# Linear attention and two mixtures of experts on one core: the old state joins the sum on TensorE, and the flag's marks are formed two steps before they are summed

## The chip, the cores and the metric

The kernel runs on one core of a Trainium2 chip. The metric is the device time of one execution in microseconds (us), the median of several runs. A core has five engines with one queue each: TensorE (PE, matrix products; its weight loads are listed as PEld), VectorE (DVE), ScalarE (ACT), GpSimd (POOL) and SyncE (SP, which issues most transfers). Each works through its queue in order and waits there for semaphores of the others.

## The reference

Three stages follow each other. Sizes: 2 batches, 8 heads, 768 positions, head width 48; 1536 tokens of width 384.

```
# attention with a decaying state, per batch and head
state = alpha[t, :, None] * state + outer(k[t], v[t])
y[t]  = q[t] @ state
# one expert of 8 for each token (384 -> 1024 -> 384), gate = softmax at the maximum
e = argmax(x @ w_gate);  out = gate * (relu(x @ w1[e]) @ w2[e])
# a dense layer (384 -> 2048 -> 384); its weights come as 64-bit floats
h = x @ w_in;  out = (h * tanh(softplus(h))) @ w_out
```

## The kernel before, in words

All instructions are put on the engines' queues in the order in which the program text issues them; no planner moves them.

**Attention.** The 1536 tokens are cut into 12 tiles of 128 positions, six for each batch (`NC_B` is 6). A loop over the tiles is software-pipelined: pass i of the loop works on several tiles at once. Below, "round i" is pass i. What round i puts on the engines:

- DVE: two of the four scans of tile i+2 (the running products of alpha, L429), the state update of tile i-1 (`state_up`, L565, L566 or L568), the other two scans, then the scaled keys and queries of tile i+1 (L466, L470), two products for tile i+2 (L448, L453, which wait for the reciprocal `r` that ACT makes from the scans), and sums for the routing. After the tiles of a group (tiles 0 to 3, 4 to 6, 7 and 8) some ten to fourteen short operations for the routing of the group come on top, in rounds 4 and 5, 7 and 8, 9 and 10.
- ACT: copies of the scores (L487), logarithm and exponential of the scans (L438, L443), the negated transposed keys `kpn` (L503), copies of results.
- POOL: the causal mask on the scores (L488).
- PE: the scores of tile i (L483), the transposes of its keys (L497), the selection and gate products of tile i-1 (L547), the product of the queries with the carried state (`attend_state`, L518), the product with the masked scores (`attend_tile`, L529), and last the new part of the state (`state_mm`, L555), eight products of keys and values into the bank `bk[7]`, which wait for `kpn`.

The carried state is `s2f`/`s2` (112 partitions by 192 values, two heads on the partitions of each of four columns of heads). In the kernel before, `state_mm(i)` writes only the new part to PSUM, and `state_up(i)`, in the next round, adds the old state to it (L565) and multiplies the sum by the tile's decay (L566). For the first tile of a batch (tiles 0 and 6) there is no old state, and one multiplication does (L568). The last tile of a batch (5 and 11) has no state update. So L565 and L566 run 8 times, for tiles 1 to 4 and 7 to 10.

**Experts.** 64 steps (8 experts, 8 parts of the hidden width each) follow. A step puts on PE nine products of the first layer (`g1`, L1011) and nine of the second layer for the step three before it (`g2`, L1028); ACT and DVE turn the first layer's result into a high and a low part (`hh` L1015, `hl` L1016). Beside this, weights are split into high and low parts (`whi` on ACT, L319; `wlo` on DVE, L325), and the 64-bit weights of the dense layer are turned into 32-bit ones (`cvt_a`, `cvt_b`), with a mark in `unfit` for any value that can't be. At the end of step 60 `cvt_marks` forms one number from all marks: DVE takes the maximum per partition (L234) and compares it with zero (`mk`, L235), PE sums `mk` over the partitions into `bk[0]` (L236), and DVE joins the sum with another flag into `slow_i` (L237), which after everything else decides whether a slow exact path runs (it doesn't here).

**Dense layer.** Its first products (`f1`, L1091) are interleaved with the experts' last three steps, 61 to 63, and write the banks 0, 1, 4 and 5 in turn; the fourth `f1`, in bank 5, comes after the experts' last `g2`. ACT's `sigma` and `cosine` (L1103, L1107, L1109) and DVE's `gated` (L1117 to L1119) follow, then the second products (`f2`, L1132).

Of the kernel before, what the change touches and what calls it, by code (L numbers as in the profile page):

```python
# [12 lines left out]
BF16 = mybir.dt.bfloat16  # L13
# [3 lines left out]
ALU = mybir.AluOpType  # L17
# [6 lines left out]
def kernel(  # L24
# [18 lines left out]
    nc = tc.nc  # L43
    ctx.enter_context(tc.manual_schedule())
    B, H, S, D = q.shape
    NT, DM = out.shape
    E = w1.shape[0]
# [3 lines left out]
    NC_B = S // C  # L51
    NTILE = NT // C
    HP = H // 2
    HS = 64
    R2 = HS + D
    SW = 2 * D + E
    KD = DM // 128
    MF = FF // 128
# [169 lines left out]
        nc.sync.dma_start(out=cvt_jobs[n][1], in_=wt.bitcast(F32))  # L228


    def cvt_marks():
        mk = const.tile([128, 1], BF16, name="mk")
        mf = const.tile([128, 1], F32, name="mf")
        nc.vector.tensor_reduce(out=mf, in_=unfit, axis=AX.X, op=ALU.max)  # L234
        nc.vector.tensor_scalar(out=mk, in0=mf, scalar1=0.0, scalar2=None, op0=ALU.is_gt)  # L235
        nc.tensor.matmul(out=bk[0][:, 0:1], lhsT=ones, rhs=mk, start=True, stop=True)  # L236
        nc.vector.scalar_tensor_tensor(  # L237
            out=slow_i, in0=bk[0][0:1, 0:1], scalar=0.0, in1=slow_f, op0=ALU.is_gt, op1=ALU.max
        )


# [99 lines left out]
    with ExitStack() as actx:  # L341
# [44 lines left out]
        misc = bk[7]  # L386
# [162 lines left out]

        def state_mm(i):  # L550
            vn, kpn = vn_t[i], kpn_t.pop(i)
            for j in range(HP):
                for r in range(2):
                    p1 = min(R2, (r + 1) * HS)
                    nc.tensor.matmul(  # L555
                        out=kv[r * HS:p1, j, :], lhsT=kpn[:, j, r * HS:p1], rhs=vn[:, (2 * j + r) * D:(2 * j + r + 1) * D],
                        start=True, stop=True, skip_group_check=True,
                    )

        def state_up(i):  # L560
            pt = pt_t.pop(i)
            sv = s2[0:R2]
            dec = pt[0:R2, :, C - 1:C].to_broadcast([R2, HP, D])
            if i % NC_B:
                nc.vector.tensor_tensor(out=sv, in0=kv[0:R2], in1=sv, op=ALU.add)  # L565
                nc.vector.tensor_tensor(out=sv, in0=sv, in1=dec, op=ALU.mult)  # L566
            else:
                nc.vector.tensor_tensor(out=sv, in0=kv[0:R2], in1=dec, op=ALU.mult)  # L568

        LAST2 = NTILE - 2  # L570
        xg_l = [
# [668 lines left out]
    for e in range(E):  # L1240
        for m in range(MF):
# [29 lines left out]
                )  # L1271
            if step == E * MF - 4:
                cvt_marks()
            if m == 5 and e + 1 < E:
                xpose(e + 1)
                if e + 2 < E:
                    gather(e + 2)
# [240 lines left out]
```

## Time and profile before

| what | value |
|---|---|
| median of 3 runs | 449.08 us (448.35 to 450.48) |
| the profiled execution | 451.67 us, of which the span from first to last instruction is 449.8 us |
| mean granted clock of TensorE | 0.966 of full speed |
| PE busy | 420.8 us (94%) |
| DVE busy | 329.1 us (73%) |
| ACT busy | 330.9 us (74%) |
| attention, the loop over tiles | from the start to about 86 us |
| experts | about 95 to 240 us |
| dense layer | about 227 us to the end |

The attention stage is a mesh of short operations on four engines with waits on each; the two stages behind it are long rows of matrix products with PE hardly idle. PE's clock has two levels, 2.4 GHz and 1.2 GHz; the profile gives the granted clock of a stretch as a share of the full one, so 0.50 is 1.2 GHz throughout. A wait is printed in brackets behind an instruction: the idle time of its engine just before it, and who ended it.

### The profile page before, as it was taken

Reading aid. Unit: us, or ns where it says so; the run is one execution under the profiler, and the core shown is the slowest. Engines: PE = TensorE matmul, PEld = TensorE weight load, DVE = VectorE, ACT = ScalarE, POOL = GpSimd, SP = SyncE. Lnnn points to the kernel's source line nnn. Section 1 sums busy time; section 2 is a strip of 40 time slices with the busy share of each in tenths; the row PEclk is TensorE's granted clock in tenths of the full one; section 3 lists DMA queues with packets and bytes.
Section 4 is the critical chain, followed back from the end, with each engine's and each line's share of the span. In section 5 each row is a group of like instructions: output and inputs, shape, how many; then the busy total and the mean of one; then the engine's idle time right before and its main releaser. Section 6 shows DMA issues by size and latency. Waiting matters only on the chain. (4 is left out here: it accounts for less than half of the span.)

```text
span 449.8 us, 8433 instructions
## 1 busy us (share of the span) xinstructions
PE 420.8 (94%) x3120; PEld 382.7 (85%) x3120; DVE 329.1 (73%) x682; ACT 330.9 (74%) x584; POOL 60.3 (13%) x74
## 2 busy tenths in 40 slices
PE   7898897899999999999899999999999999999990
PEld 3787787679999999999797989989988989988880
DVE  7899897388989999988935876976795553553750
ACT  5787777267688877867669878878878867767760
POOL 4122446112002120200000000000000000030302
PEclk9999799599999999999999999999999999999996
DMA  7999642269999999997941212112000000010102
GB/s 264 303 308 368 224 153 90 69 215 287 317 337 350 323 300 331 338 301 244 255 140 62 70 36 66 42 35 71 2 0 1 0 1 0 1 71 0 72 3 74
DMA packets 47086, 68.89 MB, mean 153 GB/s; under 512 B 5500, under 2 KB 35964, under 8 KB 47036
## 3 DMA queue, kind: packets, MB, share of 16 engines
q1 hardware_dynamic: 45116, 63.55, 45.0%
q0 software_dynamic: 1920, 4.73, 2.9%
q8 instruction: 26, 0.43, 0.4%
q14 instruction: 24, 0.20, 0.1%
HBM read 56.65 MB, written 11.61 MB: 152 GB/s over the span
## 5 line engine op out<-in xcount | busy, mean ns | idle before, releaser
L1132 PE MATMUL bk<-whi,big 128*128 128x384 f32 x384 | 106.6, 338 | 1.4 <-DVE x2l L1038 0.8
L325 DVE TENSOR_TENSOR wlo<-st,whi 128x768 fp32r<-128x768 f32 x74 | 70.0, 953 | 18.0 <-ACT whi L319 17.3
L1117 DVE TENSOR_TENSOR p<-p,bk 128x512 f32<-128x512 f32 (+1 forms) x49 | 33.0, 673 | 58.8 <-ACT p L1109 58.8
L1132 PEld LDWEIGHTS bk<-whi,big 128*128 128x128 f32 x384 | 70.5, 188 | 4.8 <-DVE x2l L1038 1.1
L1132 PE MATMUL bk<-wlo,big 128*128 128x384 f32 x192 | 64.9, 338 | 0.0
L319 ACT ACTIVATE whi<-st 128x768 fp32r<-128x768 f32 x74 | 61.7, 842 | 3.2 <-DMA st<-in_w_dram 3.2
L1103 ACT ACTIVATE p<-bk 128x512 f32<-128x512 f32 (+1 forms) x49 | 28.9, 590 | 39.6 <-PE bk L1091 39.3
L1028 PE MATMUL bk<-hl,whi 128*128 128x240 f32 x192 | 53.0, 276 | 0.1
L1028 PE MATMUL bk<-hh,wlo 128*128 128x240 f32 x192 | 52.7, 275 | 0.0
L1028 PE MATMUL bk<-hh,whi 128*128 128x240 f32 x192 | 52.7, 274 | 0.0
L100 POOL DMA_INDIRECT out_dram<-acc,srt x12 | 11.7, 973 | 241.2 <-DVE acc L1156 238.8
L1091 PE MATMUL bk<-x2l,whi 128*128 128x512 f32 (+1 forms) x147 | 41.8, 392 | 0.0
L1091 PE MATMUL bk<-x2h,wlo 128*128 128x512 f32 (+1 forms) x147 | 41.4, 390 | 0.0
L1091 PE MATMUL bk<-x2h,whi 128*128 128x512 f32 (+1 forms) x147 | 41.2, 389 | 0.0
L1015 ACT ACTIVATE hh<-bk 128x240 fp32r<-128x240 f32 x64 | 23.5, 368 | 21.8 <-PE bk L1011 21.3
L1132 PEld LDWEIGHTS bk<-wlo,big 128*128 128x128 f32 x192 | 36.0, 188 | 1.7
L1028 PEld LDWEIGHTS bk<-hl,whi 128*128 128x128 f32 x192 | 36.4, 189 | 0.3 <-DVE hl L1016 0.3
L1028 PEld LDWEIGHTS bk<-hh,whi 128*128 128x128 f32 x192 | 36.4, 190 | 0.0
L1028 PEld LDWEIGHTS bk<-hh,wlo 128*128 128x128 f32 x192 | 36.3, 189 | 0.0
L1011 PE MATMUL bk<-xh,whi 128*128 128x240 f32 x192 | 33.4, 282 | 1.7 <-DVE hl L1016 1.3
L1119 DVE TENSOR_TENSOR big<-p,big 128x512 fp32r<-128x512 f32 (+1 forms) x49 | 33.4, 682 | 1.7
L1091 PEld LDWEIGHTS bk<-x2h,wlo 128*128 128x128 f32 x147 | 27.3, 188 | 6.6
(220 smaller groups left out, 873.9 us busy)
## 6 DMA issues: line engine op xcount, KB each, us to landing
st<-in_w_dram SPq DMA_DIRECT2D x64, 384.0 KB, 7.6
qn<-in_q_t_dram SPq DMA_DIRECT2D x12, 256.0 KB, 5.8
kn<-in_k_t_dram SPq DMA_DIRECT2D x12, 256.0 KB, 5.5
w<-in_w_in_dram SPq DMA_DIRECT2D x6, 512.0 KB, 7.2
w<-in_w_out_dram SPq DMA_DIRECT2D x6, 512.0 KB, 7.3
tab<-zero SPq DMA_DIRECT2D x4, 720.0 KB, 7.0
an<-in_alpha_t_dram SPq DMA_DIRECT2D x11, 256.0 KB, 6.8
vn<-in_v_n_dram SPq DMA_DIRECT2D x12, 192.0 KB, 4.0
```

Of the source, the lines that this page charges most:

```text
L100: r = nc.gpsimd.indirect_dma_start(out=dst[:, :], out_offset=bass.IndirectOffsetOnAxis(ap=idx, axis=0), in_=src, in_offset=None, bounds_ch ...
L319: nc.scalar.activation(out=whi[i], in_=w, func=AF.Copy)
L325: nc.vector.tensor_tensor(out=wlo[i], in0=w, in1=whi[i].bitcast(F32), op=ALU.subtract)
L1011: nc.tensor.matmul(out=hps, lhsT=a[:, kk], rhs=b_[:, kk, :], start=(n == 0), stop=(n == 3 * KD - 1))
L1015: nc.scalar.activation(out=hh, in_=hps, func=AF.Relu)
L1028: nc.tensor.matmul(out=y[n], lhsT=a[:, ns], rhs=b_, start=(m == 0 and t == 0 and n % 2 == 0), stop=(m == MF - 1 and t == 2), skip_group_ch ...
L1091: r = nc.tensor.matmul(out=hps, lhsT=a[:, kk], rhs=b_[:, kk, w0:w0 + wd], start=(n == 0), stop=(n == 3 * KD - 1))
L1103: nc.scalar.activation(out=p, in_=h2_t[b], func=AF.Sigmoid, scale=-1.0)
L1117: nc.vector.tensor_tensor(out=g, in0=g, in1=h2_t.pop(b), op=ALU.mult)
L1119: nc.vector.tensor_tensor(out=gl, in0=g, in1=gh.bitcast(F32), op=ALU.subtract)
L1132: nc.tensor.matmul(out=o_t[c], lhsT=a[:, ts], rhs=b_, start=(m in (0, MA) and n == 0), stop=(m in (MA - 1, MF2 - 1) and n == 2),)
```

## The change

Two edits.

In attention, `state_mm(i)` begins, except for the first tile of a batch, with one 32-bit product of the identity with the old state into the same place of `bk[7]`; the eight products of keys and values then add to it instead of overwriting it. `state_up(i)` is one multiplication for every tile.

In the experts, forming the marks (DVE) stays at the end of step 60; the sum on PE and the operation that reads it become `cvt_flag`, at the end of step 62, and use bank 5 instead of bank 0.

```
+    mk = const.tile([128, 1], BF16, name="mk")
     def cvt_marks():
-        mk = const.tile([128, 1], BF16, name="mk")
         mf = const.tile([128, 1], F32, name="mf")
         nc.vector.tensor_reduce(out=mf, in_=unfit, axis=AX.X, op=ALU.max)
         nc.vector.tensor_scalar(out=mk, in0=mf, scalar1=0.0, scalar2=None, op0=ALU.is_gt)
-        nc.tensor.matmul(out=bk[0][:, 0:1], lhsT=ones, rhs=mk, start=True, stop=True)
+
+    def cvt_flag():
+        nc.tensor.matmul(out=bk[5][:, 0:1], lhsT=ones, rhs=mk, start=True, stop=True)
         nc.vector.scalar_tensor_tensor(
-            out=slow_i, in0=bk[0][0:1, 0:1], scalar=0.0, in1=slow_f, op0=ALU.is_gt, op1=ALU.max
+            out=slow_i, in0=bk[5][0:1, 0:1], scalar=0.0, in1=slow_f, op0=ALU.is_gt, op1=ALU.max
         )
...
         def state_mm(i):
             vn, kpn = vn_t[i], kpn_t.pop(i)
+            first = i % NC_B == 0
+            if not first:
+                nc.tensor.matmul(
+                    out=misc[0:R2, 0:HP * D], lhsT=ident[0:R2, 0:R2], rhs=s2f[0:R2, 0:HP * D], start=True, stop=False,
+                    skip_group_check=True,
+                )
             for j in range(HP):
                 for r in range(2):
                     ...
-                        start=True, stop=True, skip_group_check=True,
+                        start=first, stop=True, skip_group_check=True,
...
         def state_up(i):
             ...
-            if i % NC_B:
-                nc.vector.tensor_tensor(out=sv, in0=kv[0:R2], in1=sv, op=ALU.add)
-                nc.vector.tensor_tensor(out=sv, in0=sv, in1=dec, op=ALU.mult)
-            else:
-                nc.vector.tensor_tensor(out=sv, in0=kv[0:R2], in1=dec, op=ALU.mult)
+            nc.vector.tensor_tensor(out=sv, in0=kv[0:R2], in1=dec, op=ALU.mult)
...
             if step == E * MF - 4:
                 cvt_marks()
+            if step == E * MF - 2:
+                cvt_flag()
```

In the rows below a bank is named by its tile number: `bk_83` is `bk[0]`, `bk_88` is `bk[5]`, `bk_90` is `bk[7]`. Lines behind the edit have moved by three to seven: L555 is L564 in the changed kernel, L565 to L568 are L573, L325 is L328, L1016 is L1021, L1091 is L1096.

First place, PE at the end of round 1, before: the last products with the masked scores, the eight products of keys and values, the scores of the next tile.

```order
L529 MATMUL bk_89<-st__321,vn 64x128
L529 MATMUL bk_89<-st__321,vn 48x128
...
L555 MATMUL bk_90<-vn,kpn 64x48
L555 MATMUL bk_90<-vn,kpn 48x48
...
L483 MATMUL bk_85<-q_0_149,kp 128x128
```

The same place in the changed kernel:

```order
L532 MATMUL bk_89<-st__322,vn 64x128
L532 MATMUL bk_89<-st__322,vn 48x128
...
L557 MATMUL bk_90<-s_148,ident 112x192
L564 MATMUL bk_90<-vn,kpn 64x48
L564 MATMUL bk_90<-vn,kpn 48x48
...
L486 MATMUL bk_85<-q_0_150,kp 128x128
```

One product stands in front of the eight and needs the state, not `kpn`; nothing else moves on PE in attention.

Second place, DVE in the middle of round 2, before: the sum for the routing, two scans, the state update of tile 1, two scans, the scaled keys.

```order
L600 TENSOR_REDUCE g_lg<-bk_88 128x8
L429 SCALAR_TENSOR_TENSOR pt<-an,zc 112x128 x2
L565 TENSOR_TENSOR s_147<-bk_90,s_147 112x192
L566 TENSOR_TENSOR s_147<-s_147,pt 112x192
L429 SCALAR_TENSOR_TENSOR pt<-an,zc 112x128 x2
L466 TENSOR_TENSOR kp<-kn,rt 112x512
```

The same place in the changed kernel:

```order
L605 TENSOR_REDUCE g_lg<-bk_88 128x8
L432 SCALAR_TENSOR_TENSOR pt<-an,zc 112x128 x2
L573 TENSOR_TENSOR s_148<-bk_90,pt 112x192
L432 SCALAR_TENSOR_TENSOR pt<-an,zc 112x128 x2
L469 TENSOR_TENSOR kp<-kn,rt 112x512
```

Two operations of 112x192 have become one.

Third place, PE and DVE at the experts' steps 60 to 63. PE before, end of step 60 and begin of step 61:

```order
L1028 MATMUL bk_90<-hl,whi_3206 128x240
L236 LDWEIGHTS ones
L236 MATMUL bk_83<-mk,ones 128x1
L1011 MATMUL bk_86<-xh,whi_3322 128x240 x3
L1011 MATMUL bk_86<-xh,wlo_3323 128x240 x3
```

PE in the changed kernel, end of step 62 and begin of step 63:

```order
L1096 MATMUL bk_84<-x2h,wlo_3453 128x512 x3
L239 LDWEIGHTS ones
L239 MATMUL bk_88<-mk,ones 128x1
L1016 MATMUL bk_86<-xh,whi_3389 128x240 x3
L1016 MATMUL bk_86<-xh,wlo_3390 128x240 x3
```

DVE before, from step 60 (`hl` of step 61 is the row behind the flag):

```order
L325 TENSOR_TENSOR wlo_3514<-st_3352,whi_3513 128x768
L196 SCALAR_TENSOR_TENSOR wt<-w_3328,wt 128x384
L234 TENSOR_REDUCE mf<-unfit 128x1
L235 TENSOR_SCALAR mk<-mf 128x1
L237 SCALAR_TENSOR_TENSOR slow_i<-bk_83,slow_f 1x1
L1016 SCALAR_TENSOR_TENSOR hl<-bk_86,hh 128x240
```

DVE in the changed kernel, over the same steps to the `hl` of step 63:

```order
L328 TENSOR_TENSOR wlo_3515<-st_3353,whi_3514 128x768
L196 SCALAR_TENSOR_TENSOR wt<-w_3329,wt 128x384
L235 TENSOR_REDUCE mf<-unfit 128x1
L236 TENSOR_SCALAR mk<-mf 128x1
L1021 SCALAR_TENSOR_TENSOR hl<-bk_86,hh 128x240
...
L1021 SCALAR_TENSOR_TENSOR hl<-bk_85,hh 128x240
L328 TENSOR_TENSOR wlo_3621<-st_3478,whi_3620 128x768
L240 SCALAR_TENSOR_TENSOR slow_i<-bk_88,slow_f 1x1
L1021 SCALAR_TENSOR_TENSOR hl<-bk_86,hh 128x240
```

The sum on PE now stands behind two more steps and two `f1`; the read of the sum stands on DVE between the `wlo` of step 62 and the `hl` of step 63.

## Rows read from the trace of the kernel before

**Rows 1.** The page, part 2: TensorE's granted clock in 40 slices.
```profile
PEclk9999799599999999999999999999999999999996
```

**Rows 2.** PE, timeline of round 3 (start us, us, engine, line, operation, count, [idle before]).
```profile
26.62 1.16 PE L483 MATMUL bk<-q,kp 48*128 48x128 f32 x16
...
30.14 1.09 PE L529 MATMUL bk<-st__491,vn 128*64 128x128 f32 x16
31.36 0.67 PE L555 MATMUL bk<-vn,kpn 128*64 128x48 f32 x16
31.96 1.16 PE L483 MATMUL bk<-q,kp 48*128 48x128 f32 x16
```

**Rows 3.** ACT, timeline: the negated keys of round 3.
```profile
30.78 0.53 ACT L503 ACTIVATE kpn<-bk 128x448 f32<-128x448 f32 x1
```

**Rows 4.** PE, timeline: 32-bit products of 240 columns, at the low and the full clock.
```profile
87.19 1.85 PE L793 MATMUL bk<-hot,xg_l 128*128 128x240 f32 x4
...
93.17 1.39 PE L793 MATMUL bk<-hot_last,xg_l 128*128 128x240 f32 x6
```

**Rows 5.** DVE, timeline: the state update of tile 2, and of tile 6.
```profile
27.72 0.33 DVE L565 TENSOR_TENSOR s<-bk,s 112x192 f32<-112x192 f32 x1
...
28.37 1.12 DVE L429 TENSOR_TENSOR_SCAN pt<-an,zc 112x128 f32<-112x128 f32 x2
...
50.81 0.33 DVE L568 TENSOR_TENSOR s<-bk,pt 112x192 f32<-112x192 f32 x1
51.06 0.73 DVE L429 TENSOR_TENSOR_SCAN pt<-an,zc 112x128 f32<-112x128 f32 x2
```

**Rows 6.** PE, timeline: where it waits in rounds 5, 6 and 9.
```profile
39.90 0.18 PE L636 MATMUL bk<-oh_all,tri 128*128 128x32 bf16 x1 [0.38 <-DVE s L565]
...
42.56 1.16 PE L483 MATMUL bk<-q,kp 48*128 48x128 f32 x16 [0.17 <-DVE q L470]
...
45.41 1.11 PE L547 MATMUL bk<-sel,xt 112*128 112x104 f32 x8 [1.15 <-ACT st__755 L487]
...
49.19 0.67 PE L555 MATMUL bk<-vn,kpn 128*64 128x48 f32 x16 [1.65 <-ACT kpn L503]
...
69.05 0.67 PE L555 MATMUL bk<-vn,kpn 128*64 128x48 f32 x16 [0.89 <-ACT kpn L503]
```

**Rows 7.** ACT, timeline: its waits in rounds 6 and 8.
```profile
47.41 0.63 ACT L438 ACTIVATE ln<-pt 112x512 f32<-112x512 f32 x1 [1.60 <-DVE pt L429]
...
59.20 1.09 ACT L487 ACTIVATE st__922<-bk 128x512 f32<-128x512 f32 x2 [1.08 <-PE bk L483]
```

**Rows 8.** Windows: us, busy (instructions) of PE, PEld, DVE, ACT, POOL, clock, DMA, GB/s.
```profile
50.00:52.00 2.00, 2.00 (x21) 1.77 (x19) 2.00 (x8) 1.43 (x6) 0.00 (x0) 0.62 0.46 150
```

**Rows 9.** PE, timeline of round 7, begin and end.
```profile
49.78 1.47 PE L483 MATMUL bk<-q,kp 48*128 48x128 f32 x16
...
57.39 0.63 PE L555 MATMUL bk<-vn,kpn 128*48 128x48 f32 x16
```

**Rows 10.** Timeline at the flag, steps 60 and 61: DVE, PE, ACT.
```profile
224.08 0.55 DVE L196 SCALAR_TENSOR_TENSOR wt<-w,wt 128x384 uint32<-128x384 uint32 x1
...
224.75 0.16 DVE L235 TENSOR_SCALAR mk<-mf 128x1 bf16<-128x1 f32 x1
224.96 0.16 PE L236 MATMUL bk<-mk,ones 128*128 128x1 bf16 x1 [2.25 <-DVE mk L235]
...
226.27 0.37 ACT L1015 ACTIVATE hh<-bk 128x240 fp32r<-128x240 f32 x1 [3.16 <-PE bk L1011]
```

**Rows 11.** Timeline behind the flag: DVE's waits, and PE's fourth `f1`.
```profile
230.72 2.70 DVE L325 TENSOR_TENSOR wlo<-st,whi 128x768 fp32r<-128x768 f32 x3 [3.64 <-ACT whi L319]
...
238.50 0.96 DVE L325 TENSOR_TENSOR wlo<-st,whi 128x768 fp32r<-128x768 f32 x1 [4.76 <-ACT whi L319]
239.37 0.40 DVE L1016 SCALAR_TENSOR_TENSOR hl<-bk,hh 128x240 fp32r<-128x240 f32 x1
...
240.71 0.86 PE L1091 MATMUL bk<-x2h,whi 128*128 128x512 f32 x3
```

## The prediction

> **What bounds the kernel now.** I read the granted clock by slices first [rows 1]: it is full but for three stretches, all in the first fifth, around 10, 53 and 85 us. So the attention stage loses time to the clock as well as to waits; the two later stages run at full clock. Then the waits of PE: behind 100 us there is one above 1 us, the flag's product, 2.25 us [rows 10]. Then the timelines of the four engines in attention, round by round, to see who is late.
>
> A steady round, round 3, starts on PE at 26.62 with the scores and ends at 31.96 with the next [rows 2]: 5.34 us. In it PE works without a gap from 26.62 to 30.14 + 1.09 = 31.23, then waits 0.13 us for `kpn`, which ACT finishes at 30.78 + 0.53 = 31.31 [rows 3], and needs 31.96 - 31.36 = 0.60 for the state products. So PE has 5.21 us of work in a round of 5.34. DVE, which feeds ACT, is just as full there: it sets the 5.34 and PE is only 0.13 behind as second. That decides what the first edit can bring.
>
> **The attention edit.** DVE loses one operation in 8 rounds. From the start of L565 to the start of what follows L566 it is 28.37 - 27.72 = 0.65 us; the single multiplication from PSUM takes 51.06 - 50.81 = 0.25 the same way [rows 5]. The saving is 0.40 us a round, 1.60 for tiles 1 to 4, 1.60 for tiles 7 to 10.
>
> PE gains a 32-bit product of 192 columns. The trace has none; the nearest are those of 240 columns. Six records (a 32-bit product leaves two) span 1.39 us at full clock [rows 4], with the last one's own 0.37 taken off (1.39 - 0.37) / 5 = 0.20 each, so 0.41 a product, and by columns 0.33 for 192. At the low clock four span 1.85, about twice as much: 0.66. Bounds: below, nothing, where it fits into PE's wait for `kpn`, since it needs only the state; above, 0.41, and 0.82 at the low clock. A gain from it is excluded, it is only added work. I take 0.33 and 0.66.
>
> Rounds 2 to 4: PE's 5.21 become 5.54, 0.20 above the old round, as the 0.13 of waiting covers only part of it. PE comes three times 0.20, about 0.6 us, later into round 5. DVE meanwhile gains its 0.40 in each. It needs PE's state products only at its `state_up`: L565 of tile 2 starts at 27.72 [rows 5], 1.1 us after PE, done with them, began round 3 at 26.62 [rows 2]. That slack shrinks by 0.2 + 0.4 a round; it holds for the first two, and the routing on DVE in round 4 adds to it for the rest. Queued behind the product on PE are the state products and the next scores, and for these waits ACT; that is the 0.6.
>
> Round 5 is DVE's: PE waits 0.38 for it before the rank products and 0.17 before the next scores [rows 6]. These waits end earlier now and take up PE's 0.6, so PE starts round 6 about where it did, at 42.56, while DVE and the scans are 1.60 earlier. There ACT waits 1.60 for the scans [rows 7] and PE then 1.65 for `kpn` [rows 6]. Both shrink: `kpn` comes 1.6 earlier, and so do the state products and the scores of round 7, at about 48.2 for 49.78.
>
> What follows depends on the clock. In the trace it is full until 50 and 0.62 in 50 to 52 [rows 8]; round 7 on PE takes 57.39 - 49.78 = 7.61 to its state products [rows 9], where the same work in round 3 takes 31.36 - 26.62 = 4.74. Before the fall PE was idle 1.15 us before L547 and 1.65 before L555 [rows 6]. With the change L555 starts at 49.19 - 1.6 = 47.6; L529 ahead of it ended at 49.19 - 1.65 = 47.54 and can end some 0.4 earlier, by its mask, which hangs on PE's scores (unmoved) and on ACT (sooner free): an idle time of 0.5 in place of 1.65, an estimate from these rows. Other single waits, such as 0.89 in round 9 [rows 6], were not followed by a fall. So I expect the clock to stay full here. Round 7 then runs 48.2 + 4.61 + 0.33 = 53.1 to its state products (`kpn` is there at about 52.9), 4.2 earlier than 57.39. The rounds behind are led by ACT and DVE, which were themselves late for round 7's sake: ACT waits 1.08 for PE's scores in round 8 [rows 7]. I put 4.0 us at the end of the stage; in rounds 8 to 10 the identity product lies under waits like the 0.89 or costs what DVE's second 1.60 pays.
>
> The Trainium skill ("TensorE: Matmul & The Clock Gate", section "HAM oscillation") has a rule that speaks against this: it takes a long idle gap of PE to lower the clock, short ones do not. By that rule 1.65 us would not be what lowered it and shortening it returns nothing; the time would be the 446.0 of the first rival. The trace is against it: the clock fell with no wait above 1.65 near.
>
> **The experts edit.** PE stands 2.25 us before the flag's product, because DVE reaches `mk` only at 224.75, behind the conversion at 224.08 [rows 10]. That wait goes: `mk` is ready long before its new place. What is late next? ACT waits 3.16 us for PE's first-layer product of step 61 [rows 10], so it does not stand in the way; DVE, 2.2 us behind PE at this point, idles 3.64 before the `wlo` of step 61 [rows 11], so it catches up without the pause; `hl` is needed three steps later. All work up to the fourth `f1` is led by PE's `f1` results and shifts with it. The new place: the read of the sum waits on DVE behind the `wlo` at 238.50, itself waiting for ACT, and stands ahead of `hl` at 239.37, for which PE's last `g2` waits [rows 11]. It takes 0.1 us there, PE's wait grows by that. The fourth `f1` writes the same bank at 240.71 [rows 11], 1.3 us behind the read: no wait. Bounds: 0 to 2.25 gained, up to 0.15 lost. I take 2.25 - 0.15 = 2.1.
>
> **Sum.** The profiled execution took 451.67 us, 1.87 around its span of 449.8. 451.67 - 4.0 - 2.1 = 445.6; it was 2.59 above the median, so beside the median 449.08 - 6.1 = 443.0.
>
> **Rivals.**
> 1. The low clock of round 7 stays. Then the 1.6 us lead meets the identity product at the low clock: 1.6 - 0.66 = 0.94 remain, with 2.1 that is 3.04: 446.0. For it: three low stretches in the trace, PE still with two gaps in round 6, and executions need not fall alike. The skill says so too (same page, section "What's actually happening": the monitored stretches run free of the program).
> 2. The flag's wait only moves: DVE's backlog, no longer let off by the pause, reaches PE at some `hl`. It takes back 2.1: 445.1. For it: DVE is 2.2 behind at 224.75. Against: its 3.64 of idle time.
> 3. Slower: the identity product is on PE's path in all 8 rounds, seven at 0.33 and one at 0.66, 2.97 us, and DVE's saving buys nothing since PE, not DVE, sets every round. It decides where PE's round is above DVE's: 5.54 against 5.34 - 0.40. If round 5's slack is not given to PE, that is 2.97 later, and if the low stretch begins one round earlier or ends one later, another 7.61 - 4.74 = 2.9. Without the second: 449.08 + 2.97 - 2.1 = 449.95; with it, 452.8. For it: PE's gapless 4.61 us in round 3. Against: PE's waits of 0.38, 1.65 and 0.89 on others.
>
> **Chances.** The forecast 0.48, rival 1 0.30, rival 2 0.11, rival 3 0.11 (0.06 of it with the low stretch). The likeliest's own range is 441.8 to 444.6 (0.41 for 0.33, half of round 7's gain). To hold 8 in 10 it must reach rival 1 and part of rival 3: 441.4 to 448.4. A difference of 0.5%, 2.2 us, is about what a measurement of this kernel can tell from none. Below 446.8 lie the forecast, rival 2 and some two thirds of rival 1 less a margin for what I have not seen: 0.70. Within 0.5%: 0.24. Slower: 0.06.
>
> **What would show it.** Right: in the changed profile PE's rounds 2 to 4 take about 5.5 us, DVE's about 4.95 of work with idle time new in it; the wait for `kpn` in round 6 is about 0.5; the slices around 53 us show full clock; no wait of PE at the flag, and the first `f1` follows its `g2` without a pause. Wrong: PE's wait for `kpn` in round 6 stays above 1.3 or the clock falls there all the same (rival 1); a new wait of PE on `hl` at steps 61 to 63 (rival 2); rounds 7 to 10 longer than before (rival 3).

## The result and the profile after

The changed kernel takes 447.44 us in the median (444.72 to 459.04, 20 runs), the kernel before, run beside it, 452.65 (448.35 to 454.62, 20 runs). The ratio is 0.9894, 95% interval 0.9868 to 0.9921: faster by 1.06%, which is 4.8 us of 452.65. Of each kernel's runs those more than 1.5% above its fastest, here only the 459.04, are left out of the ratios. The forecast, 443.0 of 449.08, was a ratio of 0.9865 (6.1 us). The sign was right, the size too large by a quarter, and the reasons, as the traces below show, wrong in the larger of the two terms.

The profiled execution took 445.37 us, span 443.5, against 451.67 and 449.8 before: 6.3 us less. The page's clock line after, beside that of [rows 1]:

```profile
PEclk8999999999999999999999999999999999999996
```

The dips around 53 and 85 us are gone. Round 3 on TensorE's timeline, which answers to [rows 2]:

```profile
27.17 1.16 PE L486 MATMUL bk<-q,kp 48*128 48x128 f32 x16
...
30.70 1.09 PE L532 MATMUL bk<-st__493,vn 128*64 128x128 f32 x16
31.72 0.58 PE L557 MATMUL bk<-s,ident 112*112 112x192 f32 x2
32.23 0.67 PE L564 MATMUL bk<-vn,kpn 128*64 128x48 f32 x16
32.82 1.16 PE L486 MATMUL bk<-q,kp 48*128 48x128 f32 x16
```

The round takes 32.82 - 27.17 = 5.65 us, 5.34 before, and no row of it shows a wait. The new product holds TensorE for 32.23 - 31.72 = 0.51 us. ScalarE in the same round, and beside it VectorE (the timeline of each):

```profile
28.42 1.09 ACT L490 ACTIVATE st__493<-bk 128x512 f32<-128x512 f32 x2 [1.87 <-PE bk L486]
29.39 0.63 ACT L441 ACTIVATE ln<-pt 112x512 f32<-112x512 f32 x1
30.06 0.63 ACT L446 ACTIVATE r<-ln 112x512 f32<-112x512 f32 x1
```

```profile
27.29 0.36 DVE L573 TENSOR_TENSOR s<-bk,pt 112x192 f32<-112x192 f32 x1 [0.27 <-PE bk L564]
...
30.72 0.69 DVE L451 TENSOR_TENSOR er<-pt,r 112x512 f32<-112x512 f32 x1 [1.24 <-ACT r L446]
...
33.22 0.73 DVE L432 TENSOR_TENSOR_SCAN pt<-an,zc 112x128 f32<-112x128 f32 x2
33.87 0.67 DVE L469 TENSOR_TENSOR kp<-kn,rt 112x512 f32<-112x512 f32 x1
...
36.37 0.69 DVE L451 TENSOR_TENSOR er<-pt,r 112x512 f32<-112x512 f32 x1 [1.24 <-ACT r L446]
...
40.47 1.10 DVE L469 TENSOR_TENSOR kp<-kn,rt 112x512 f32<-112x512 f32 x1
41.49 1.11 DVE L473 TENSOR_TENSOR q<-qn,pt 112x512 f32<-112x512 f32 x1
...
45.28 2.13 DVE L432 TENSOR_TENSOR_SCAN pt<-an,zc 112x128 f32<-112x128 f32 x4
```

Read the two together. VectorE has time to spare, but spends it waiting 1.24 us for `r`; ScalarE forms `r` behind its copies of the scores (L490), and the copies wait for TensorE. At its state update (27.29) VectorE waits for TensorE's state products as well. So VectorE is tied to TensorE's round, in rounds 3 and 4 alike (30.72 to 36.37 is again 5.65).

The 1.24 is more than the 0.40 saved. Two further operations of the round have become shorter: the second pair of scans takes 0.73 us, 1.12 before [rows 5], and the scaled keys 0.67, 1.05 before (first line below). Before, they ran beside GpSimd's mask selection (28.54 to 29.93); now (29.09 to 30.57) it falls on the end of the scaled queries and on VectorE's wait.

In round 5 it goes the other way. There the multiplications for keys and queries take 1.10 and 1.11 us. In the kernel before they took 0.66 and 0.68 (its timeline of VectorE, rounds 3 and 5):

```profile
29.41 1.05 DVE L466 TENSOR_TENSOR kp<-kn,rt 112x512 f32<-112x512 f32 x1
...
41.25 0.66 DVE L466 TENSOR_TENSOR kp<-kn,rt 112x512 f32<-112x512 f32 x1
41.83 0.68 DVE L470 TENSOR_TENSOR q<-qn,pt 112x512 f32<-112x512 f32 x1
```

The difference is what runs beside them: after the change GpSimd's two mask selections lie over both (its timeline; the first line is round 2):

```profile
22.80 2.21 POOL L491 TENSOR_SCALAR_AFFINE_SELECT st__411<-st__411 128x512 f32<-128x512 f32 x2 [4.92 <-ACT st__411 L490]
...
40.39 1.67 POOL L491 TENSOR_SCALAR_AFFINE_SELECT st__667<-st__667 128x512 f32<-128x512 f32 x2 [4.17 <-ACT st__667 L490]
```

Before, they ended at 40.73, ahead of the multiplications. The Trainium skill ("SBUF — State Buffer", section "SBUF: two separate sides") says that a VectorE operation with two SBUF inputs and a GpSimd operation that reads SBUF exclude each other, and the second waits; the trace agrees, with 0.44 and 0.43 us more for the two. The scans ahead of them gain, 0.73 us at 39.83 for 1.17 at 40.16 before, so round 5 loses 0.4 net, which is all that its own shorter state update saves.

In round 2 it is GpSimd that is held up: its selection takes 2.21 us, 1.34 before, and TensorE waits for it:

```profile
25.06 1.07 PE L532 MATMUL bk<-st__411,vn 128*48 128x128 f32 x14 [0.22 <-POOL st__411 L491]
```

The round takes 27.17 - 20.89 = 6.28 us, 0.63 more than rounds 3 and 4, and 5.29 before.

Round 6 on TensorE and ScalarE, which answer to [rows 6, 7]:

```profile
45.51 1.11 PE L550 MATMUL bk<-sel,xt 112*128 112x104 f32 x8 [0.69 <-ACT st__756 L490]
...
49.29 0.67 PE L564 MATMUL bk<-vn,kpn 128*64 128x48 f32 x16 [1.65 <-ACT kpn L506]
49.88 1.16 PE L486 MATMUL bk<-q,kp 48*128 48x128 f32 x16
...
56.17 1.16 PE L486 MATMUL bk<-q,kp 48*128 48x128 f32 x16
```

```profile
47.51 0.63 ACT L441 ACTIVATE ln<-pt 112x512 f32<-112x512 f32 x1 [1.54 <-DVE pt L432]
```

The scans of tile 8 begin at 45.28 (45.18 before; counted from the scores of round 2 they come 0.54 later), ScalarE waits 1.54 for them (1.60), TensorE 1.65 for `kpn` (1.65). Only the wait at 45.51 is shorter, 0.69 for 1.15, and there TensorE itself comes later. The lead that the prediction built on is not there. Yet round 7 ran at the full clock; the window that answers to [rows 8]:

```profile
50.00:52.00 2.00, 2.00 (x26) 1.88 (x27) 2.00 (x8) 1.73 (x6) 0.19 (x1) 1.00 0.51 140
```

Round 7 took 56.17 - 49.88 = 6.29 us, from 8.17 before. The other low stretch that is gone lies in the tail, from the scores of round 11 to the first expert product. On TensorE:

```profile
75.24 1.16 PE L486 MATMUL bk<-q,kp 48*128 48x128 f32 x16 [0.80 <-DVE q L473]
...
89.23 0.64 PE L1016 MATMUL bk<-xh,whi 128*128 128x240 f32 x3 [0.38 <-ACT xh L1005]
...
130.82 0.60 PE L1016 MATMUL bk<-xh,whi 128*128 128x240 f32 x3 [1.64 <-DVE hl L1021]
...
218.75 0.50 PE L1016 MATMUL bk<-xh,whi 128*128 128x240 f32 x3
```

The tail takes 89.23 - 75.24 = 13.99 us; before it was 94.95 - 76.43 = 18.52, at 1.2 GHz from about 78 to 91. Of the 6.3 us, 4.5 come from there. The lead at the first expert product is 5.72; by step 60 it has shrunk to 3.8 (216.73 against 220.52). Most of that stands at one place: TensorE arrives earlier at weights that are not earlier by as much, and the 1.64 at 130.82 goes back to a conversion on ScalarE that stands 2.49 us for its transfer:

```profile
127.54 0.85 ACT L322 ACTIVATE whi<-st 128x768 fp32r<-128x768 f32 x1 [2.49 <-DMA st<-in_w_dram]
```

The flag is as predicted. At 218.75 step 61 follows without the wait of 2.25 [rows 10], and the lead is 6.2 again. Its mark is formed at 220.95, long before its sum, and VectorE still has idle time behind it [rows 11]:

```profile
220.95 0.16 DVE L236 TENSOR_SCALAR mk<-mf 128x1 bf16<-128x1 f32 x1
...
224.44 2.69 DVE L328 TENSOR_TENSOR wlo<-st,whi 128x768 fp32r<-128x768 f32 x3 [3.02 <-ACT whi L322]
```

### The profile page after: what moved, and what is told of

It is laid out like the page before. It is cut to its first block, busy times and chain, and to the rows that moved or that the text cites. A ratio compares the mean times of both kernels' runs of the same rounds, so it can differ in the third digit from the quotient of the medians.

```text
span 443.5 us, 8459 instructions
## 1 busy us (share of the span) xinstructions
PE 417.4 (94%) x3134; PEld 378.5 (85%) x3136; DVE 324.6 (73%) x674; ACT 330.3 (74%) x584; POOL 62.5 (14%) x74
## 5 line engine op out<-in xcount | busy, mean ns | idle before, releaser
L328 DVE TENSOR_TENSOR wlo<-st,whi 128x768 fp32r<-128x768 f32 x74 | 70.0, 953 | 18.8 <-ACT whi L322 18.2
L1096 PE MATMUL bk<-x2l,whi 128*128 128x512 f32 (+1 forms) x147 | 41.9, 393 | 0.0
L1096 PE MATMUL bk<-x2h,wlo 128*128 128x512 f32 (+1 forms) x147 | 41.4, 390 | 0.0
L1096 PE MATMUL bk<-x2h,whi 128*128 128x512 f32 (+1 forms) x147 | 41.2, 389 | 0.0
L1016 PE MATMUL bk<-xh,whi 128*128 128x240 f32 x192 | 33.6, 283 | 2.9 <-DVE hl L1021 2.6
L1096 PEld LDWEIGHTS bk<-x2h,wlo 128*128 128x128 f32 x147 | 27.3, 188 | 6.7
```

The costliest lines, as they stand in the source:

```text
L328: nc.vector.tensor_tensor(out=wlo[i], in0=w, in1=whi[i].bitcast(F32), op=ALU.subtract)
L1016: nc.tensor.matmul(out=hps, lhsT=a[:, kk], rhs=b_[:, kk, :], start=(n == 0), stop=(n == 3 * KD - 1))
L1096: r = nc.tensor.matmul(out=hps, lhsT=a[:, kk], rhs=b_[:, kk, w0:w0 + wd], start=(n == 0), stop=(n == 3 * KD - 1))
```

## The experiments

The theory after reading the trace, A: the flag's wait is worth its 2.25 us; the attention edit by itself costs TensorE time, and what it gives is a clock that stays at 2.4 GHz more often. The rival, B: the saved VectorE operation is the gain, as predicted. Kernels of one group ran on one chip beside the same runs of the kernel before; ratios are to these, with their 95% interval. "Low time" is worked out from each run's mean granted clock c and span as 2 (1 - c) span, the time at 1.2 GHz that this clock amounts to, and given as the mean over the runs that count; the 52 such runs of before listed beside the experiments have 24.0 us, the changed kernel's 16.1. In those 52 a us of low time goes with 0.27 us of device time (correlation 0.88).

The table has, from each profiled execution, the time between the starts of the scores of two rounds (2 to 4 together, 5 and 6, 7, 8 to 10) and the tail; a star marks stretches with a fall to 1.2 GHz.

| kernel | 2-4 | 5-6 | 7 | 8-10 | tail | low time | median us | ratio |
|---|---|---|---|---|---|---|---|---|
| before | 15.95 | 12.50 | 8.17* | 18.48 | 18.52* | 24.0 | 452.65 | 1 |
| after | 17.58 | 11.41 | 6.29 | 19.07 | 13.99 | 16.1 | 447.44 | 0.9894 [0.9868, 0.9921] |
| e1 flag edit only | 15.96 | 12.49 | 5.55 | 19.47 | 16.90* | 22.2 | 447.74 | 0.9919 [0.9875, 0.9963] |
| e2 attention edit only | 17.58 | 11.73* | 9.98* | 18.63 | 13.99 | 17.9 | 451.40 | 0.9954 [0.9918, 0.9990] |
| e3 no old state | 15.83 | 11.86 | 5.54 | 18.71 | 16.86* | 24.4 | 450.32 | 0.9966 [0.9929, 1.0003] |
| e4 product and VectorE | 17.42 | 11.93* | 9.94* | 18.69 | 14.00 | 19.5 | 450.98 | 1.0029 [0.9981, 1.0076] |
| e5 before, filler | 15.94 | 12.48 | 5.54 | 19.46 | 14.02 | 9.4 | 447.41 | 0.9899 [0.9854, 0.9944] |
| e6 after, filler | 17.57 | 11.41 | 6.29 | 20.02 | 13.98 | 8.3 | 446.46 | 0.9884 [0.9837, 0.9932] |
| e7 flag edit, filler | 15.95 | 12.48 | 5.54 | 19.47 | 13.99 | 13.7 | 444.70 | 0.9851 [0.9806, 0.9896] |
| e8 product in 7-10 only | 15.96 | 12.48 | 6.29 | 19.60 | 14.01 | 17.2 | 446.65 | 0.9925 [0.9885, 0.9965] |
| e9 half the product | 17.77 | 11.50 | 8.67* | 18.49 | 13.99 | one run | 445.44 | - |
| e10 flag edit, `kpn` first, filler | 15.94 | 11.27 | 6.41 | 19.53 | 13.99 | 9.1 | 444.09 | 0.9839 [0.9779, 0.9899] |
| e11 after, `kpn` first | 17.56 | 10.18 | 6.41 | 18.97 | 16.44* | 12.9 | 444.44 | 0.9847 [0.9783, 0.9911] |
| e12 e11 and filler | 18.20 | 10.19 | 6.42 | 18.98 | 13.99 | 10.3 | 444.66 | 0.9870 [0.9821, 0.9919] |

### One part of the change alone (e1, e2)

e1 keeps the old `state_mm` and `state_up`; of the change only this stands:

```diff
+    mk = const.tile([128, 1], BF16, name="mk")
...
+            if step == E * MF - 2:
+                cvt_flag()
```

> Only the experts edit: the marks at the end of step 60, their sum and its read at the end of step 62 in bank 5; attention as before. If the wait at the flag is simply gone (my prediction): 2.1 to 2.4 us faster than before, PE without a wait at steps 60 to 63, attention unchanged. If the wait only moves (rival 2): no faster, and a wait of PE on an hl of about 2 us at steps 61 to 63.

e2 is the other half, with the flag as before:

```diff
+                nc.tensor.matmul(out=misc[0:R2, 0:HP * D], lhsT=ident[0:R2, 0:R2], rhs=s2f[0:R2, 0:HP * D], start=True, stop=False, ...)
-                nc.vector.tensor_tensor(out=sv, in0=kv[0:R2], in1=sv, op=ALU.add)
```

> Only the attention edit; the flag as before. The theory of the prediction (DVE runs ahead by 0.4 us a round and the clock stays up): 4 us faster. The theory that the changed profile suggests (PE's round sets the stage because ACT, which waits for PE's scores, hands DVE its next input; the identity product costs PE 0.5 us a round): rounds 2 to 4 of 5.65 us for 5.34, round 6 begins 0.5 later than before, and any gain, about 2.5 to 3 us in the median, comes from stretches of low clock that are shorter or missing.

The flag edit alone gave 0.81% [0.37, 1.25], the attention edit 0.46% [0.10, 0.82]. The flag edit so holds most of the gain: 3.6 us [1.7, 5.6], of which the wait is 2.25. The rest lies, at least in part, behind the wait: in three of the five profiles that have it (e2, e3, e5) the clock falls to 1.2 GHz within 1.4 us of its end. In e2's (TensorE's timeline) the three products of an `f1` take 1.50 us there and 0.85 once the clock is back:

```profile
225.44 0.16 PE L236 MATMUL bk<-mk,ones 128*128 128x1 bf16 x1 [2.25 <-DVE mk L235]
...
228.19 1.50 PE L1093 MATMUL bk<-x2h,whi 128*128 128x512 f32 x3
...
230.54 0.85 PE L1093 MATMUL bk<-x2h,wlo 128*128 128x512 f32 x3
```

From the first product of step 61 to that of step 62 these three take 5.6 to 5.8 us, before and e4 4.2; in none of the nine profiles with the flag edit does the clock fall between 212 and 236 us. Some 1.5 us in three of five are 0.9 on the mean, which with the 2.25 makes 3.2 of the 3.6.

For the attention edit compare e1 with the changed kernel in the table, both at full clock from round 2 to 10: 53.47 us without it and 54.35 with it. It loses 1.62 in rounds 2 to 4 (0.99 of it in round 2, where TensorE waits for GpSimd), regains 1.08 in 5 and 6, where TensorE waits less because it comes later, loses 0.74 in 7 and regains 0.40 in 8 to 10. So in these two executions it costs 0.9 us, and a gain must lie elsewhere. Nor is a gain in the whole kernel's time firm: the intervals of e1 and of the changed kernel overlap, and the plain means of e2's 12 runs and of the 35 of before beside them are 451.6 and 451.7 us. In e2's execution the clock did fall in round 7, in spite of the edit (TensorE's timeline):

```profile
49.22 0.99 PE L561 MATMUL bk<-vn,kpn 128*64 128x48 f32 x16 [1.65 <-ACT kpn L503]
50.14 2.08 PE L483 MATMUL bk<-q,kp 48*128 48x128 f32 x16
...
58.58 0.98 PE L554 MATMUL bk<-s,ident 112*112 112x192 f32 x2
59.49 0.70 PE L561 MATMUL bk<-vn,kpn 128*64 128x48 f32 x16
```

At 1.2 GHz the product costs 59.49 - 58.58 = 0.91 us and the round 9.98: the edit makes such a round dearer.

### The two halves of the attention edit (e3, e4)

e3 leaves out the addition of the old state altogether: no VectorE operation and no product.

```diff
-            if i % NC_B:
-                nc.vector.tensor_tensor(out=sv, in0=kv[0:R2], in1=sv, op=ALU.add)
-                nc.vector.tensor_tensor(out=sv, in0=sv, in1=dec, op=ALU.mult)
-            else:
-                nc.vector.tensor_tensor(out=sv, in0=kv[0:R2], in1=dec, op=ALU.mult)
+            nc.vector.tensor_tensor(out=sv, in0=kv[0:R2], in1=dec, op=ALU.mult)
```

> The kernel before with the addition of the old state left out altogether (the state is lost from tile to tile): DVE's saving alone, without the product on PE. Theory of the prediction: DVE leads by 1.6 us at round 6, 1.6 to 4 us faster. Theory of the loop through ACT: rounds 2 to 4 can shrink only from 5.34 to PE's 5.21, so 0.4 us there; rounds 5 to 8 with their routing work on DVE give up to 0.4 each: 1 to 2 us faster at equal clock.

e4 adds the product to the kernel before and lets the products behind it overwrite it; VectorE keeps both operations.

```diff
+            if i % NC_B:
+                nc.tensor.matmul(out=misc[0:R2, 0:HP * D], lhsT=ident[0:R2, 0:R2], rhs=s2f[0:R2, 0:HP * D], start=True, stop=True, ...)
```

> The kernel before with the identity product put in front of the state products but overwritten by them, so DVE keeps both its operations: the cost on PE alone. Theory of the prediction (0.33 us a product, partly under waits): rounds 2 to 4 of 5.54 us, about 0.6 us slower at round 5, all of it taken up in round 5, so 0 to 1 us slower. Theory of the loop: 0.51 us a product and rounds of 5.72, 1.1 us later at round 5, of which round 5 can give back some 0.5; with the later rounds 1 to 2 us slower at equal clock. If busier PE alone keeps the clock up, it is no slower or even faster.

Round 3 on TensorE in e3:

```profile
26.32 1.16 PE L483 MATMUL bk<-q,kp 48*128 48x128 f32 x16
...
31.34 1.16 PE L483 MATMUL bk<-q,kp 48*128 48x128 f32 x16
```

Without either operation the round takes 5.02 us and rounds 2 to 10 take 51.94: the VectorE operation is worth 53.47 - 51.94 = 1.5 us where nothing replaces it. That is the value of the saving in these two executions, both at full clock, to be set against the product's cost of 1.5 + 0.9 = 2.4. Even here GpSimd is held up in round 2 (2.21 us), which takes 5.54. By the whole kernel's time neither can be told from the kernel before, as both intervals reach 1; e3's low time is 24.4 us, that of before, and its tail ran at 1.2 GHz. e4's tail ran at full clock, as e2's had, with a product whose result is thrown away; its rounds 2 to 4 took 17.42, 1.5 longer than before, where 1.1 was expected. That TensorE's clock, and not VectorE's time, is what the product changes was the idea behind the next three.

### Filler instead of the product (e5, e6, e7)

Filler is a burst of bf16 products of 512 columns with an output that nobody reads (`keep_busy`, a helper that the kernel already uses elsewhere). The same three bursts go into the kernel before (e5), the changed kernel (e6) and e1 (e7): in round 11 behind `check_all`, in round 10 behind `route_rank_mm`, in round 6 ahead of `state_mm`.

```diff
+                keep_busy(bk[1], 6)
...
+                keep_busy(bk[1], 4)
...
+            if i == NC_B:
+                keep_busy(bk[2], 6)
```

> The kernel before with 16 more bf16 filler products on TensorE (6 in round 6 where TensorE waits 1.65 us for kpn, 4 in round 10, 6 in round 11 behind the check), nothing else changed. Theory A (the identity product acts on the median mostly as filler: it keeps TensorE's granted clock up in round 7 and in the tail): low-clock time per run falls from the 26 us that the runs of before show on the mean to 15 to 18 us and, at the 0.4 us per low us that those runs show, the median falls by 3 to 4 us, to about 448.5. Theory B (the gain of the attention edit is the VectorE operation that it takes out): filler gains nothing, within 1 us of the kernel before.

> The changed kernel with the same filler. Theory A: its low time is already 17.5 us on the mean, so the filler takes off less, 1 to 2 us: 445.5 to 446.5. It stands 1 to 2 us below the kernel before with filler, which is the flag edit's 2.3 us less the 1 us that the attention edit costs at equal clock. Theory B: 4 us or more below the kernel before with filler.

> The flag edit alone, old attention, with the same filler. Theory A: at an equal clock the attention edit costs about 1 us (rounds 2 to 10 took 54.35 us with it and 53.47 without, both at full clock), so this kernel is the fastest of all, about 445, 0.5 to 1.5 us below the changed kernel with filler. Theory B: 1 to 3 us above the changed kernel with filler.

Filler alone, which computes nothing, took 1.01% [0.56, 1.46] off the kernel before: as much as the whole change. Low time fell from 24.0 to 9.4 us, more than the 15 to 18 that A gave. In e5's round 6 TensorE works through what was idle time, and round 7 stays at full clock (its timeline, and the page's clock line, where the one dip, around 220 us, is that behind the flag's wait):

```profile
48.42 1.47 PE L750 MATMUL bk<-busy 128*128 128x512 bf16 x6
50.14 0.67 PE L555 MATMUL bk<-vn,kpn 128*64 128x48 f32 x16 [0.25 <-ACT kpn L503]
50.73 1.16 PE L483 MATMUL bk<-q,kp 48*128 48x128 f32 x16
```

```profile
PEclk9999999999999999999899999999999999999996
```

With the clock held up in all three (low time 8 to 14 us), e6 is only 0.95 us below e5 and e7 is 1.8 below e6, in the order that A gave and B excludes: the flag edit gains, the attention edit costs. With six runs each the intervals of the three ratios overlap, so the cost rests on the traces more than on these times. A part of e6's cost is the filler itself, which in round 10 lies on TensorE's path (76.76 to 77.72, the next scores right behind it), without the wait of 0.80 that the changed kernel has there. Rounds 8 to 10 take 20.02 there, 19.07 in the changed kernel. Between the two at equal clock stand 0.9 us of the edit and 0.95 of filler: the 1.8.

### The product only where TensorE waits (e8), and half of it (e9)

```diff
-            first = i % NC_B == 0
+            first = i < NC_B + 1
...
+            if 0 < i < NC_B:
+                nc.vector.tensor_tensor(out=sv, in0=kv[0:R2], in1=sv, op=ALU.add)
+                nc.vector.tensor_tensor(out=sv, in0=sv, in1=dec, op=ALU.mult)
```

> The changed kernel with TensorE adding the old state only in rounds 7 to 10; rounds 1 to 4 add it on VectorE as before. Theory A (in rounds 1 to 4 TensorE is the engine without idle time once it has the product, 5.65 us per round against 5.34): rounds 3 and 4 take 5.34 us again, the scores of round 5 begin 1.0 to 1.3 us earlier, the low time stays as in the changed kernel (its filler effect is in the later rounds), and the median is 0.5 to 1.5 us below the changed kernel's 447.4. Theory B (VectorE's saved operation is worth having in rounds 1 to 4): 1 us or more slower than the changed kernel.

e8's rounds 2 to 4 are back at 15.96 us, as expected, but rounds 5 and 6 are back at 12.48, and the median of 446.65 has a ratio whose interval overlaps the changed kernel's. Of the 1.62 lost in rounds 2 to 4 some 1.07 come back in rounds 5 and 6, which VectorE ends, so moving the product away from there saves little. Inconclusive as to the time. The scores of round 5 came 1.62 earlier, counted from round 2, where 1.0 to 1.3 were expected: round 2, without a wait for GpSimd here, is the difference.

```diff
-  out=misc[0:R2, 0:HP * D], ... rhs=s2f[0:R2, 0:HP * D]
+  out=misc[0:R2, 0:HP * D // 2], ... rhs=s2f[0:R2, 0:HP * D // 2]
```

> The changed kernel with half of the identity product: 96 of its 192 columns (the old state of the other two head pairs is left out). Theory A (in rounds 1 to 4 TensorE has no idle time, so the round is as long as its work, and VectorE's saved operation turns into a wait for ScalarE's r): rounds 3 and 4 take 0.2 to 0.3 us less than the 5.65 of the changed kernel, 5.35 to 5.45, VectorE's wait for r falls from 1.24 to about 1.0, and the scan of tile 8 begins 0.5 to 1.0 us earlier against the scores of round 2. Theory B (the chain through ScalarE's masks and r sets the round): rounds 3 and 4 stay at 5.6 or more.

A partial miss. TensorE's and VectorE's timelines of e9, round 4:

```profile
32.42 0.44 PE L557 MATMUL bk<-s,ident 112*112 112x96 f32 x2
32.78 0.67 PE L564 MATMUL bk<-vn,kpn 128*64 128x48 f32 x16
33.38 1.16 PE L486 MATMUL bk<-q,kp 48*128 48x128 f32 x16
...
38.88 1.16 PE L486 MATMUL bk<-q,kp 48*128 48x128 f32 x16
```

```profile
36.93 0.69 DVE L451 TENSOR_TENSOR er<-pt,r 112x512 f32<-112x512 f32 x1 [1.24 <-ACT r L446]
```

Half the columns cost 0.36 us, not 0.26, so the round falls to 5.50 and not below 5.45, and VectorE's wait for `r` stays at 1.24 to the hundredth. Rounds 3 and 4 follow TensorE's work (A), but the wait isn't a measure of TensorE's surplus, as I had it: VectorE's `state_up` follows the end of the state products, `r` the scores, so both ends of the wait move with TensorE's round. The chain is one loop, and in these rounds TensorE leads it. Round 2 is again GpSimd's: its selection takes 2.82 us and the round 6.76.

### Taking the 1.65 us away (e10, e11, e12)

In round 6 ScalarE now forms `kpn` ahead of the logarithm for tile 8, which is what holds it up:

```diff
+            if i == NC_B:
+                k_neg(i)
             if far and i:
                 decay_ln(i + 2)
...
-            if carry:
+            if carry and i != NC_B:
                 k_neg(i)
```

e11 is this on the changed kernel; e10 on e7, without the burst of round 6; e12 is e11 with the burst in round 11 (`keep_busy(bk[1], 6)` behind `check_all`).

> The flag edit with the old attention and filler in rounds 10 and 11 only; in round 6 ScalarE forms kpn ahead of the logarithm for tile 8 instead of behind it. Theory A (the 1.65 us of round 6 come from ScalarE's order alone, kpn standing behind an ln that waits 1.5 us for the scan of tile 8): kpn is ready 2 us earlier, the wait in front of the state's products falls below 0.5, the scores of round 7 begin 1.0 to 1.5 us earlier against those of round 6 (5.9 instead of 7.2 us), no later round gives it back, round 7 runs at full clock without filler, and the median is 1 us below the flag edit with three bursts of filler, 443.5 to 444. Theory B (round 7 waits for VectorE anyway): round 6 stays at 7 us or round 7 grows by as much, no gain.

> The changed kernel, and in round 6 ScalarE forms kpn ahead of the logarithm for tile 8. Theory A: the 1.65 us that the changed kernel still waits there go, round 6 takes 5.5 instead of 6.8 us, the median falls by 1 to 2 us to 445.5 to 446.5, which is what the prediction had hoped to get from VectorE's lead. Theory B: no gain, the wait moves to the scores of round 7 or to the second half of the masks.

> The changed kernel with kpn formed ahead of the logarithm in round 6 and six filler products in round 11 behind the check, where TensorE waits 1.56 us for the routing of the next tile. Theory A (identity product alone doesn't hold the clock in the tail; the profiled run without filler was at 1.2 GHz from 80.3 to 87.9; filler holds it): the tail from the scores of round 11 to the first expert product takes 14.0 us, the low time falls from 12.9 us to under 9 on the mean, and the median is 0.5 to 1.5 us below the kernel without the filler, 443 to 444. Theory B (what is gained ahead of the experts is given back there, where the weights' transfers set the pace): within 0.5 us of the kernel without filler's 444.4.

e11's ScalarE and TensorE, round 6:

```profile
45.99 0.55 ACT L506 ACTIVATE kpn<-bk 128x448 f32<-128x448 f32 x1
47.64 0.63 ACT L441 ACTIVATE ln<-pt 112x512 f32<-112x512 f32 x1 [1.10 <-DVE pt L432]
```

```profile
47.60 0.62 PE L564 MATMUL bk<-vn,kpn 128*48 128x48 f32 x16
48.79 1.16 PE L486 MATMUL bk<-q,kp 48*128 48x128 f32 x16 [0.57 <-DVE q L473]
```

`kpn` comes 2.7 us earlier (45.99 for 48.71), the wait of 1.65 becomes one of 0.57 on VectorE, and rounds 5 and 6 shrink from 11.41 to 10.18, of which round 7 and the later ones keep nearly all: rounds 2 to 10 take 53.12 for 54.35. The ratio 0.9847 [0.9783, 0.9911] lies below the changed kernel's, though the intervals overlap. e10 got the same 1.2 us in round 6 but gave 0.87 of it back in round 7, where TensorE now waits for `kpn` (its timeline), a miss of A:

```profile
55.53 0.67 PE L558 MATMUL bk<-vn,kpn 128*64 128x48 f32 x16 [0.83 <-ACT kpn L506]
```

e12 held the tail at full clock (13.99 us for e11's 16.44) and gained nothing, 444.66 for 444.44, within B's 0.5. But the two profiles don't show B's reason: from the first expert product to the end e12 takes 352.5 us, e11 352.0. What e12 gains in the tail it has lost ahead of it: its scores of round 2 begin 1.35 later, and round 2 is 0.63 longer, where GpSimd's selection takes 2.82 us for 2.20. Why the start differs (20.8 to 22.6 us to the scores of round 2, the five kernels with filler in round 11 the latest) is not shown. At some 444 to 445 us e7, e10, e11 and e12 stand together, on three chips; whether the later stages hold them there is not shown.

## Why the prediction was right in sign and off in its reasons

**What bounds a steady round: half right.** It was right that TensorE stands only just behind VectorE. Its work was read too high: the 5.21 counts the end of the products with the masked scores in full, though the next ones start before it. Where nothing waits, the round takes 5.65 - 0.51 = 5.14 without the product, and 5.02 in e3, so TensorE stood 0.2 to 0.3 behind, not 0.13. What was missing is that with the product it stands ahead, and that VectorE's lead can't grow then.

**Cost of the product: mis-sized.** 0.33 was taken, with 0.41 as the upper bound; it is 0.51, and 0.91 at 1.2 GHz for 0.66. The error was to scale by columns: e9's 96 columns took 0.36, so 0.21 of the 0.51 doesn't depend on them. By rounds it is 5.65 - 5.02 = 0.63.

**"DVE and the scans are 1.60 earlier": this step failed.** The saving of 0.40 a round is real on VectorE; in rounds 3 and 4 it became, with the 0.8 that no longer goes to the overlap with GpSimd, a wait of 1.24 for `r`, which hangs on TensorE's scores by way of ScalarE's copies, and in round 5 a net 0.4 more overlap used up that round's own 0.40. The prediction had the first half of this loop before it (VectorE needs TensorE's state products at `state_up`, and "that slack shrinks by 0.2 + 0.4 a round") and did not follow the other half, from the scores over the copies to `r`. The first half fails too: the slack of 1.1 us was to hold for two rounds, and already round 3's state update, at 27.29, waits 0.27 for TensorE. GpSimd's selection, held up by VectorE in rounds 2 and 7, stands in no term of the sum. Hence the scans of tile 8 came at 45.28 and not 1.6 earlier, and the wait of 1.65 in round 6 stayed.

**TensorE's lateness into round 5, "taken up" there: right in kind.** It was 1.62 us instead of 0.6 (0.3 in each of rounds 3 and 4, 0.99 in round 2), and rounds 5 and 6 took up 1.08.

**The clock, 4.2 us: right in the profiled run, but not by the edit's hand.** The step was that a shorter wait keeps the clock up in round 7. The wait stayed at 1.65, and the clock stayed up: that was luck. Over all profiles: of the eight in which TensorE waits 1.64 or 1.65 for `kpn` in round 6, the clock fell there in four (before, e2, e4, e9) and not in four (after, e1, e3, e8), with product or without; of the six in which the wait was filled or moved away (e5, e6, e7, e10 to e12) it fell in none. So the link that the prediction drew, from the wait to the clock, is likely real (four of eight against none of six; after the flag's 2.25 three of five), but as a matter of chance from execution to execution, and the edit left the wait as it was. The Trainium skill ("TensorE: Matmul & The Clock Gate", section "What's actually happening") has the observation that sets the clock run free of the program; four against four at the same wait agrees with that. The size was off too: from round 2 to 10 the low stretch cost 55.10 - 53.47 = 1.6 us in the kernel before, since rounds 8 to 10 give back 1.0 of the 2.6 that round 7 loses.

**What was not seen: the tail.** Its low stretch, worth 4.5 us, is the largest single piece of the 6.3. Without product or filler the profiles show it in three of three, with the product in one of six, with filler in round 11 in none of five. That the product takes part in it is likely by these counts and by the low times: over the 53 runs of after, e2, e4 and e8, which have the product and no filler, the mean is 17.5 us, over the 23 of e1 and e3, which have neither, 23.2, a difference of 5.8 with a standard error of 1.4. What in round 10 or 11 it changes is not settled. The wait of TensorE ahead of the scores of round 11 is one candidate, 1.14 in the three profiles without product or filler and 0.53 to 0.94 in the six with the product; e11, which has the product, 0.80 there and a low tail, shows that it is no guarantee.

**The flag: right.** 2.25 us gone, no new wait behind it, VectorE idle 3.02 there. e1's 3.6 [1.7, 5.6] holds the 2.1 forecast. That the clock can fall behind the wait was not seen.

**Rivals.** Rival 1 (the low clock of round 7 stays) is what e2 ran into. Rival 3's ground, TensorE, not VectorE, setting the round, is what happened in rounds 3 and 4; in 2 and 7 it was TensorE with 0.22 of waiting for GpSimd. Its price was 0.9 us net and not 2.97, since rounds 5 and 6 and 8 to 10 gave part of it back.

**The sum.** Low time fell by 7.9 us, at 0.27 each 2.1; the flag's 2.25; less 0.9 for the product: 3.5 us of the 4.8 [3.6, 6.0] measured. About 1.3 stay unaccounted for; the 0.27 is a slope over runs and the 0.9 comes from one pair of executions, so the parts are no closer than that. The term of 4.0 for attention came out at about 1.2: the 4.8 of both edits less e1's 3.6, or 2.1 less 0.9. e2 by itself has 2.1 [0.4, 3.7] by its ratio and nothing by the plain means, so it isn't clear of zero.

## What to carry to other kernels

Before counting an operation taken off a full engine as time, follow the loop that this engine stands in right round, through every queue, and ask which engine leads once the work has moved: here TensorE was 0.2 to 0.3 us behind and led at once. Look also at what the engine's other work will then run beside: here GpSimd's selection moved, and with it 0.4 to 0.8 us a round. Where the granted clock shows falls, run the kernel with filler in the waits ahead of them first: it costs a few lines, and here it gained as much as the whole change. A wait that stands because of one engine's program order (`kpn` behind a logarithm that isn't due) is best removed in that order.

## What the runs showed of the chip

A two-input VectorE multiplication of 112x512 takes 0.66 to 0.69 us alone and 1.05 to 1.12 beside GpSimd's mask selection, whose pair takes 1.3 to 1.7 where VectorE waits for it and up to 2.8 (e9, e12) where it is the one held up. So a small shift in the order can cost or save 0.4 to 0.9.

The same kernel's runs spread over 446 to 455 us, and the mean granted clock of a run tells most of it (correlation 0.88 over the 52 runs). A wait of TensorE of 1.65 us (round 6) was followed by a fall of the clock in four of eight profiles, one of 2.25 us (the flag) in three of five. One profile of before and one of after can differ by several us for this alone: the profiled pair's 6.3 us held 4.5 of it in the tail.

What is gained ahead of the experts is partly lost there: in the profiles with the flag edit the time from the first expert product to the end is 352.0 to 355.0 us, and TensorE's waits for `hl` in it, behind conversions that wait for weights, sum to 0.7 to 2.6 us, the largest sums in the three that ran longest (after, e7, e8).
